# A new issue order for the first third of a fused recurrence and FFN kernel: decays of rounds 1 and 2 in quarters, no products of zeros

## The chip, the cores and the metric

The kernel runs on one core of one Trainium2 chip. The metric is the device time of one execution in microseconds (us). The time before is 322.89 us, the median of 3 runs.

## The reference

The first half is a gated linear recurrence in chunks of 32 positions; its result y, as 3072 rows of 256, goes through a two-layer FFN with a softplus between.

```
for c in range(nc):                                  # 24 chunks of 32
    cum = np.cumsum(la, axis=-1)                     # la = log(clip(a))
    L = np.exp(cum[..., :, None] - cum[..., None, :]) * causal
    y_intra = einsum('bhij,bhjd->bhid', einsum('bhin,bhjn->bhij', Cc, Bc) * L, xc)
    y_inter = einsum('bhin,bhnd->bhid', Cc, state) * exp(cum)[..., None]
    y[:, :, sl] = y_intra + y_inter
    state = decay_full * state + sum_j(Bc * xc * decay_from_j)
h = x @ w_in                                         # x: 3072 x 256, w_in: 256 x 2048
g = np.maximum(h, 0.0) + np.log1p(np.exp(-np.abs(h)))
return g @ w_out                                     # w_out: 2048 x 256
```

There are 4 batches, 8 heads, 768 positions, head dimension 32 and state dimension 16.

## The kernel before

The 768 positions are cut into 6 rounds of 128 (index u or j). A round holds 4 batches times 128 positions, that is 512 tokens, which is the width of one matmul. The FFN's hidden dimension of 2048 is cut into 16 tiles of 128 (index k). Each fp32 operand of the FFN is split into a high and a low part of type fp32r, and each product is made of three matmuls (high by high, high by low, low by high). So one step `F j.k` (first layer) is 6 matmuls of 512 columns, and one step `Z j.k` (second layer) is 6 as well; in 96 such pairs lies most of TensorE's work.

The recurrence of a round, for each half p of the batches: `D u.p` writes the decay weights into the tile `rm` (GpSimd, `affine_select`); `S u.p` makes the scores on TensorE (tile `sp`, 4 PSUM banks); `M u.p.q` multiplies a quarter of them into `rm` (VectorE); `I u.p` applies them to x (TensorE, tile `yp`). `B`, `U`, `N`, `T`, `C`, `R` scale, update and read the state (tiles `bp`, `zp`, `tb`, `td`, `cc`, `yp`). `G` multiplies by the growth factors `gg`, and `Xh`, `Xl` split the result into `xh`, `xl` for the FFN.

`W s` splits 512 KB of a weight matrix that `w s` has loaded: four operations of ScalarE and two of VectorE, in six stages, one each time the word stands in the order (even s: `w_in`, for the tiles k = s and s+1; odd s: `w_out`, tiles k = s-1 and s). `P j.k` takes a tile through softplus (`e`, ScalarE), its high part (`gh`, ScalarE) and its low part (`gl`, VectorE). `H0`, `H1` are the first halves of `F0.0` and `F0.1`. `ft`, `fr`, `gq`, `growth`, `gd`, `gg` prepare decay and growth factors: `growth` is made on chip, `gd` stores it to DRAM and `gg u` loads it back broadcast. `warm n` issues n matmuls of a zero tile (`some`), whose result nobody reads.

The order of the first third is written out by hand in `ORDER`, one word for each step. The instructions are kept in that order on each engine, and the DMAs on SP's queue as well. All compute engines take their instructions strictly in order, so a step that waits holds up everything behind it on its engine. After the words of `ORDER` a regular loop runs the steps s = 32 to 99, with the recurrence of rounds 3 to 5 put in by `FILLS`; the change does not touch it.

Buffers that matter: PSUM tiles of tag `ps` have 6 slots, shared by `sp` (4 at a time), `yp` (2), `zp`, `hp` and the small setup products; `rm` has 2 (`RM`), so the decays of round 1 wait for the `I` of round 0, and those of round 2 for the `I` of round 1; `wraw` has 4 (`WRAW`), so a later `w` waits for the third ScalarE stage of an earlier `W`; `un` has 2, so the load of round 3 waits for the readers of round 1.

The function `decays` takes a quarter k or none, so the change needs no new code:

```
ks = slice(0, KP) if k is None else slice(k * KP // 4, (k + 1) * KP // 4)
```

Of the kernel before, what the change touches and what calls it, by code (L numbers as in the profile page):

```python
# [55 lines left out]


ORDER = """
la warm1 warm1 loga loga gb warm4 logr logr ft0 ft0 gq0 gq0 ft0 ft0 ft0 growth D0.0.2 kb D0.0.3 growth ft0 fr0 fr0
warm1 us0.0 D0.0.1 D0.0.0 S0.0 w14 w6 M0.0.1 us0.1 warm1 D0.1.2 D0.1.1 W14 D0.1.3 M0.0.0 ux0.0 warm1 ft1 warm1 growth  # L60
w0 un1.0 M0.0.3 W14 ux0.1 w2 W6 W6 M0.0.2 W14 S0.1 W14 D0.1.0 M0.1.0 warm1 ft1 I0.0 D1.0 warm1 warm1 W14 W6 fr0 warm1
W14 W0 W0 M0.1.2 M0.1.1 fr1 w1 fr1 G0.0 gq1 fr1 W0 M0.1.3 ft1 W0 warm1 fr1 Xh0.0 ft1 Xl0.0 fr0 un1.1 gq1 I0.1 G0.1 W0
warm1 Xh0.1 W0 S1.0 tl W6 W6 Xl0.1 M1.0.0 warm1 M1.0.3 H0 W6 H1 F0.1 W2 W2 B0.0 F0.0 P0.1 M1.0.1 W2 M1.0.2 gd W2 P0.1
P0.1 F0.7 P0.0 W2 W2 P0.7 B0.1 w4 W4 F0.6 gg1 S1.1 C1 P0.0 D1.1 M1.1.2 P0.6 P0.0 F0.3 F0.2 M1.1.3 M1.1.0 W1 U0 P0.6 W1
w8 I1.0 warm1 W1 P0.3 M1.1.1 w3 N0 W1 W4 B1.0 B1.1 I1.1 warm1 gg3 W1 P0.6 w5 W1 W4 T1 W3 W4 W4 U1 W3 warm1 W3 w7 w10
R1 P0.2 Z0.0 G1.0 W4 W3 P0.3 P0.2 G1.1 W3 W3 Z0.1 F0.5 W5 F0.4 P0.2 P0.3 Xh1.1 W7 Xh1.0 F0.14 N1 W7 Z0.2 Xl1.1 Xl1.0
F1.2 W5 W5 P0.4 F1.1 un2.1 W5 w12 un3.1 W7 P0.4 P0.4 F1.4 gg2 W5 P0.5 P0.5 W7 F1.7 W5 P1.1 W7 W7 Z0.3 W12 F1.3 P0.5
W12 P0.7 P0.7 Z0.4 w11 Z0.5 W8 W8 W8 W12 P1.2 W8 Z0.6 F1.0 W12 P1.3 Z0.7 W12 P1.1 P1.1 W8 P1.0 F1.6 un3.0 K0.0 F1.5
P1.2 W8 P1.3 W10 W10 D2.0 P1.0 P1.0 w9 W10 W10 F0.8 K0.1 Z1.0 P1.6 W10 W10 Z1.1 P1.3 P1.2 P1.4 F0.10 P1.4 P1.5 P1.5
un2.0 C2 Z1.2 F0.9 B2.1 W11 Z1.3 P1.5 W12 P1.4 P1.6 P1.6 P0.9 P0.9 W9 P0.9 W11 W11 W11 T2 P0.10 P1.7 Z1.4 P0.8 Z1.5  # L70
Z1.6 P1.7 P1.7 F0.13 W9 W9 W9 S2.0 Z1.7 P0.8 P0.14 D2.1 W9 P0.10 F0.11 M2.0.1 F1.12 B2.0 W11 M2.0.0 P0.8 M2.0.3 P0.14
K1.1 W11 F1.10 w13 K1.0 P0.10 W9 W13 P1.10 w15 M2.0.2 P0.11 Z0.8 W13 W13 P0.14 Z0.9 W15 P0.11 P0.11 Z0.10 S2.1 M2.1.1
W13 P0.13 F0.15 W15 W15 F0.12 M2.1.0 P0.12 P0.12 P0.12 F1.15 P0.13 M2.1.2 Z0.11 W13 W15 P0.15 W15 P0.13 F1.8 P1.8
F1.11 W15 P1.10 W13 Z0.12 F1.9 P1.10 P0.15 Z0.13 P1.8 F1.14 P1.14 P1.8 P1.9 Z0.14 P0.15 P1.9 Z0.15 P1.9 P1.11 M2.1.3
U2 I2.0 E0 P1.14 P1.14 I2.1 R2 G2.1 Z1.8 Z1.9 G2.0 Z1.10 P1.12 P1.15 P1.12 P1.11 Xh2.0 P1.11 P1.12 Xh2.1 Xl2.1 Xl2.0
F1.13 P1.13 P1.15 N2 P1.15 Z1.11 P1.13 P1.13
"""
HALF = NFT // 2
AHEAD = 32
# [770 lines left out]
```

## Time and profile before

| | us |
|---|---|
| median of 3 runs | 322.89 |
| the profiled execution's own time | 322.9 |
| its span, first to last instruction | 320.8 |
| TensorE busy | 311.4 (97%) |
| ScalarE busy | 169.4 (53%) |
| VectorE busy | 165.3 (52%) |
| GpSimd busy | 33.8 (11%) |

Lines of the profile give an engine, the line of the kernel, the operation and its tiles as output<-inputs. PE is TensorE's matmuls, PEld its weight loads, DVE VectorE, ACT ScalarE, POOL GpSimd, SP the queue that issues the DMAs. Line 131 is the helper through which all instructions of the ordered part go, so the tiles tell them apart. Matmuls overlap, so a row's duration is longer than the distance to the next matmul. About 2.1 us of the time lie outside the span.

### The profile page before, as it was taken

The page shows a single profiled execution, that of the slowest core. Times are in us where ns is not written, and L with a number is a line of the kernel's source. Part 1 is how long each engine was busy: PE and PEld are TensorE (multiplying, and loading weights), DVE is VectorE, ACT ScalarE, POOL GpSimd, SP SyncE. Part 2 cuts the span into 40 slices and gives each one's busy share as a digit, 9 for nine tenths or more (in the row PEclk, how much of TensorE's full clock was granted, in tenths as well). Part 3 has the DMA queues.
Part 4 walks back from the last instruction along what each step waited for, and adds up shares of the span by engine and source line. Part 5 has one row for each costly group of instructions (what it writes and reads, how often), then busy time and mean ns, then how long its engine had stood idle before and what let it go on. Part 6 is the DMA issues. An engine that isn't in the chain of part 4 may idle for free.

```text
span 320.8 us, 5643 instructions
## 1 busy us (share of the span) xinstructions
PE 311.4 (97%) x2328; PEld 252.2 (79%) x2328; DVE 165.3 (52%) x254; ACT 169.4 (53%) x290; POOL 33.8 (11%) x35
## 2 busy tenths in 40 slices
PE   8989699999999999999999999999999999999996
PEld 5677478888888878888888888888888888888885
DVE  4899974474835793455762344372344342322222
ACT  5989398878764453443254534344633444544450
POOL 5730600000000230000410000230000000000000
PEclk9999999999999999999999999999999999999999
DMA  7968449611000242100250100000100000100001
GB/s 219 406 249 231 134 163 310 246 67 65 2 0 0 77 189 65 65 3 0 73 193 0 65 2 0 2 2 0 65 3 0 2 1 2 65 0 0 2 0 65
DMA packets 10297, 24.36 MB, mean 76 GB/s; under 512 B 1056, under 2 KB 1696, under 8 KB 10272
## 3 DMA queue, kind: packets, MB, share of 16 engines
q1 hardware_dynamic: 10272, 24.01, 21.6%
q8 instruction: 18, 0.29, 0.4%
q14 instruction: 7, 0.06, 0.0%
HBM read 20.76 MB, written 3.24 MB: 75 GB/s over the span
## 4 chain that ended last, share of the span: by engine, by line
PE 85%; DVE 10%; issue 2%; ACT 2%; POOL 1%; DVEq 0%; POOLq 0%; ACTq 0%
PE acc L131 38%; PE hp L131 37%; PE sp L131 3%; PE yp L131 3%; DVE gl L131 3%; DVE rm L131 1%; PE end L131 1%; DVE bp L400 1%; PE warm L131 1%; PE fp L131 1%; DVE w L131 1%; DVE bp L131 1%; DVE wil L131 1%; POOL kc L131 1%; PE gp L131 1%
## 5 line engine op out<-in xcount | busy, mean ns | idle before, releaser
L617 DVE TENSOR_TENSOR gl<-e,gh 128x512 fp32r<-128x512 f32 x62 | 42.9, 692 | 100.1 <-ACT gh L614 100.1
L611 ACT ACTIVATE e<-hp 128x512 f32<-128x512 f32 x62 | 37.1, 599 | 90.4 <-PE hp L131 90.0
L131 PE MATMUL hp<-xh,wil 128*128 128x512 f32 (+1 forms) x196 | 75.5, 385 | 1.1 <-DVE wil L131 1.1
L131 PE MATMUL hp<-xl,wih 128*128 128x512 f32 (+1 forms) x196 | 75.6, 386 | 0.3 <-DVE xl L131 0.3
L131 PE MATMUL hp<-xh,wih 128*128 128x512 f32 (+1 forms) x196 | 75.8, 387 | 0.0
L131 PE MATMUL acc<-gh,woh 128*128 128x512 f32 x188 | 74.7, 397 | 0.0
L131 PE MATMUL acc<-gh,wol 128*128 128x512 f32 x188 | 73.3, 390 | 1.1 <-DVE wol L131 1.1
L131 PE MATMUL acc<-gl,woh 128*128 128x512 f32 x188 | 73.5, 391 | 0.6 <-DVE gl L131 0.6
L131 PEld LDWEIGHTS hp<-xh,wil 128*128 128x128 f32 x196 | 36.8, 188 | 8.6 <-DVE wil L131 1.3
L131 PEld LDWEIGHTS hp<-xl,wih 128*128 128x128 f32 x196 | 36.8, 188 | 7.9 <-DVE xl L131 0.7
L131 PEld LDWEIGHTS hp<-xh,wih 128*128 128x128 f32 x196 | 36.8, 188 | 7.7 <-ACT xh L131 0.2
L131 PEld LDWEIGHTS acc<-gh,wol 128*128 128x128 f32 x188 | 35.3, 188 | 8.8 <-DVE wol L131 1.5
L131 PEld LDWEIGHTS acc<-gh,woh 128*128 128x128 f32 x188 | 35.3, 188 | 8.8 <-issue 0.9
L131 PEld LDWEIGHTS acc<-gl,woh 128*128 128x128 f32 x188 | 35.3, 188 | 8.0 <-DVE gl L131 1.0
L614 ACT CAST gh<-e 128x512 fp32r<-128x512 f32 x62 | 38.5, 621 | 5.2 <-PE acc L131 3.3
L131 DVE TENSOR_TENSOR gl<-e,gh 128x512 fp32r<-128x512 f32 x34 | 27.3, 814 | 23.8 <-ACT gh L131 23.7
L131 ACT ACTIVATE e<-hp 128x512 f32<-128x512 f32 x34 | 19.5, 590 | 18.4 <-PE hp L131 10.1
L131 POOL TENSOR_SCALAR_AFFINE_SELECT rm<-fc 128x512 f32<-128x512 f32 (+1 forms) x13 | 18.0, 1408 | 89.8 <-PE yp L131 84.5
L131 ACT CAST gh<-e 128x512 fp32r<-128x512 f32 x34 | 20.6, 617 | 7.3 <-PE acc L131 7.1
L131 ACT ACTIVATE signs<-wraw 128x512 f16<-128x512 f32 (+1 forms) x32 | 23.2, 775 | 0.0
L356 POOL TENSOR_SCALAR_AFFINE_SELECT rm<-fc 128x2048 f32<-128x2048 f32 x5 | 13.0, 2625 | 86.0 <-PE yp L131 86.0
L131 DVE TENSOR_TENSOR rm<-sp,rm 128x512 f32<-128x512 f32 x24 | 15.7, 680 | 2.5 <-PE sp L131 2.4
(93 smaller groups left out, 229.8 us busy)
## 6 DMA issues: line engine op xcount, KB each, us to landing
un<-in_un SPq DMA_DIRECT2D x10, 768.0 KB, 5.8
wraw<-in_w_in SPq DMA_DIRECT2D x8, 512.0 KB, 6.4
wraw<-in_w_out SPq DMA_DIRECT2D x8, 512.0 KB, 4.2
gg<-gd SPq DMA_DIRECT2D x20, 128.0 KB, 3.9
out_t<-o SPq DMA_DIRECT2D x9, 256.0 KB, 2.1
head_in_h<-in_un SPq DMA_DIRECT2D x2, 384.0 KB, 6.4
head_in_l<-in_un SPq DMA_DIRECT2D x2, 384.0 KB, 8.5
out_t<-half SPq DMA_DIRECT2D x2, 256.0 KB, 2.5
```

What stands on the lines that cost most here:

```text
L131: return lambda *a, **k: tc.keep_in_program_order(f(*a, **k))
L356: Pl.affine_select(out=weights_of(u, p)[:, ks].rearrange("p h (c i) -> p (h c) i", i=SUB), in_=fs.rearrange("p h c -> p (h c)").unsqueeze( ...
L400: V.tensor_tensor(bp, home(u, p)[:, U_B:].rearrange("p (h n) -> p h n", n=N), f_tok[u][0][:, p * KP : (p + 1) * KP].unsqueeze(2).broadcast ...
L611: A.activation(e, h, AF.Softplus)
L614: A.copy(gh, e)
L617: V.tensor_tensor(gl, e, gh.bitcast(F32), op=ALU.subtract)
```

## The change

Only the text of `ORDER` changes. Against the old one it has the same steps, with two differences in what is issued: the 17 `warm` words (20 matmuls of zeros) are all gone, and the four whole decays `D1.0`, `D1.1`, `D2.0`, `D2.1` are each replaced by four quarters, `D1.0.0` to `D2.1.3`. Everything else is permuted. The beginning and the stretch up to the first products of round 1's FFN, before and after:

```diff
-la warm1 warm1 loga loga gb warm4 logr logr ft0 ft0 gq0 gq0 ft0 ft0 ft0 growth D0.0.2 kb D0.0.3 growth ft0 fr0 fr0
-warm1 us0.0 D0.0.1 D0.0.0 S0.0 w14 w6 M0.0.1 us0.1 warm1 D0.1.2 D0.1.1 W14 D0.1.3 M0.0.0 ux0.0 warm1 ft1 warm1 growth
-w0 un1.0 M0.0.3 W14 ux0.1 w2 W6 W6 M0.0.2 W14 S0.1 W14 D0.1.0 M0.1.0 warm1 ft1 I0.0 D1.0 warm1 warm1 W14 W6 fr0 warm1
-W14 W0 W0 M0.1.2 M0.1.1 fr1 w1 fr1 G0.0 gq1 fr1 W0 M0.1.3 ft1 W0 warm1 fr1 Xh0.0 ft1 Xl0.0 fr0 un1.1 gq1 I0.1 G0.1 W0
-warm1 Xh0.1 W0 S1.0 tl W6 W6 Xl0.1 M1.0.0 warm1 M1.0.3 H0 W6 H1 F0.1 W2 W2 B0.0 F0.0 P0.1 M1.0.1 W2 M1.0.2 gd W2 P0.1
-P0.1 F0.7 P0.0 W2 W2 P0.7 B0.1 w4 W4 F0.6 gg1 S1.1 C1 P0.0 D1.1 M1.1.2 P0.6 P0.0 F0.3 F0.2 M1.1.3 M1.1.0 W1 U0 P0.6 W1
-w8 I1.0 warm1 W1 P0.3 M1.1.1 w3 N0 W1 W4 B1.0 B1.1 I1.1 warm1 gg3 W1 P0.6 w5 W1 W4 T1 W3 W4 W4 U1 W3 warm1 W3 w7 w10
-R1 P0.2 Z0.0 G1.0 W4 W3 P0.3 P0.2 G1.1 W3 W3 Z0.1 F0.5 W5 F0.4 P0.2 P0.3 Xh1.1 W7 Xh1.0 F0.14 N1 W7 Z0.2 Xl1.1 Xl1.0
...
+la loga loga ft0 logr us0.0 w0 logr gb ft0 kb S0.0 ux0.0 W0 growth gq0 us0.1 growth ux0.1 D0.0.0 W0 M0.0.0 ft0 D0.0.1
+W0 M0.0.1 D0.0.2 D0.0.3 M0.0.2 M0.0.3 D0.1.0 fr0 fr0 ft0 I0.0 ft0 D1.0.2 ft0 D0.1.2 gq0 W0 B0.0 D0.1.1 S0.1 w2 B0.1 U0
+G0.0 M0.1.0 gq1 fr1 M0.1.2 N0 M0.1.1 D0.1.3 M0.1.3 W0 ft1 W2 Xh0.0 fr0 D1.0.0 W0 fr1 un1.0 W2 I0.1 Xl0.0 gq1 G0.1 ft1
+w4 S1.0 D1.1.0 W2 fr0 W2 D1.1.2 ft1 W4 W4 M1.0.2 ft1 Xh0.1 w1 H0 H1 fr1 un1.1 w7 Xl0.1 W4 growth D1.0.1 B1.0 W2 W2 w6
+gd F0.1 fr1 D1.1.1 tl F0.0 F0.2 W4 P0.1 W4 P0.0 P0.2 M1.0.1 gg1 D1.0.3 B1.1 M1.0.3 M1.0.0 W4 F0.3 P0.0 S1.1 W1 P0.0 W1
+W6 W6 D1.1.3 w3 F0.5 W1 P0.1 W6 M1.1.1 F0.4 M1.1.0 P0.4 M1.1.3 M1.1.2 U1 W1 C1 W6 P0.1 I1.0 D2.0.0 W1 W6 w5 W1 I1.1 R1
+Z0.0 G1.1 W3 D2.1.0 W3 D2.1.1 P0.2 G1.0 D2.0.2 P0.2 Z0.1 P0.3 D2.0.3 un2.0 W6 W3 W3 P0.5 w12 S2.0 M2.0.0 un2.1 Xh1.0
+W7 W7 W3 M2.0.2 F0.7 W3 D2.1.2 W7 W7 un3.1 P0.3 P0.3 P0.4 F0.6 Xh1.1 W5 Xl1.0 Z0.2 D2.1.3 W5 W5 Xl1.1 T1 P0.5 P0.6 N1
...
```

## Rows read from the trace of the kernel before

**Rows 1.** The page, engines' busy time, then TensorE in 40 slices and its granted clock

```profile
PE 311.4 (97%) x2328; PEld 252.2 (79%) x2328; DVE 165.3 (52%) x254; ACT 169.4 (53%) x290; POOL 33.8 (11%) x35
...
PE   8989699999999999999999999999999999999996
...
PEclk9999999999999999999999999999999999999999
```

**Rows 2.** The chain that ended last, in order of time: start, duration

```profile
46.96 5.53 PE hp L131 x23
...
59.29 1.36 PE hp L131 x6
...
118.19 2.79 PE acc L131 x11
```

**Rows 3.** TensorE's waits in the first 125 us: total, times, longest

```profile
PE zp L131 <- DVE bp L131: 1.6, 1, 1.6
PE hp L131 <- DVE wil L131: 1.1, 1, 1.1
PE acc L131 <- DVE wol L131: 1.1, 1, 1.1
...
PE acc L131 <- DVE gl L131: 0.6, 1, 0.6
...
PE hp L131 <- DVE xl L131: 0.3, 1, 0.3
```

**Rows 4.** TensorE in order of time, 0 to 47 us: start, duration, count

```profile
0.98 3.17 PE L131 MATMUL warm<-some 128*32 128x512 bf16 x6 [0.98 <-POOL some L131]
4.18 1.53 PE L131 MATMUL fp<-both_logs,kc 128*128 128x96 f32 x8
...
9.16 1.13 PE L131 MATMUL fp<-both_logs,kc 128*128 128x96 f32 x8
...
19.16 0.39 PE L131 MATMUL hp<-xh,wih 128*128 128x256 f32 x1
...
30.36 0.43 PE L131 MATMUL zp<-head_in_h,bp 128*32 128x64 f32 x16
...
36.62 0.50 PE L131 MATMUL acc<-gh,woh 128*128 128x512 f32 x1
```

**Rows 5.** All products of zeros, by their tile: nanoseconds, least/median/most

```profile
L131 PE MATMUL warm<-some x20: 376/390/631, 1.0 to 35.3; 128*32 128x512 bf16 x20
```

**Rows 6.** GpSimd and VectorE in order of time, 6 to 37 us

```profile
6.23 5.59 POOL L131 TENSOR_SCALAR_AFFINE_SELECT rm<-fc 128x512 f32<-128x512 f32 x8 [1.69 <-ACT fc L131]
...
8.56 2.48 DVE L131 TENSOR_TENSOR rm<-sp,rm 128x512 f32<-128x512 f32 x4 [1.30 <-PE sp L131]
...
17.76 2.40 POOL L131 TENSOR_SCALAR_AFFINE_SELECT rm<-fc 128x2048 f32<-128x2048 f32 x1 [1.67 <-DVE xl L131]
18.36 2.33 DVE L131 TENSOR_TENSOR wil<-w,wih 128x512 fp32r<-128x512 f32 x1
...
32.04 5.20 POOL L131 TENSOR_SCALAR_AFFINE_SELECT rm<-fc 128x2048 f32<-128x2048 f32 x2 [11.88 <-PE yp L131]
32.05 2.93 DVE L131 TENSOR_TENSOR bp<-un,ft 128x256 f32<-128x256 f32 x2
...
34.90 2.86 DVE L131 TENSOR_TENSOR gl<-e,gh 128x512 fp32r<-128x512 f32 x1
```

**Rows 7.** A group of instructions by line: total us, mean ns of one, idle before

```profile
L617 DVE TENSOR_TENSOR gl<-e,gh 128x512 fp32r<-128x512 f32 x62 | 42.9, 692 | 100.1 <-ACT gh L614 100.1
```

**Rows 8.** DMA: the store of the growth factors and two others, KB, us to landing

```profile
wraw<-in_w_out SPq DMA_DIRECT2D x8, 512.0 KB, 4.2
...
out_t<-half SPq DMA_DIRECT2D x2, 256.0 KB, 2.5
...
gd<-both_logs SPq DMA_DIRECT2D x1, 96.0 KB, 8.8
```

**Rows 9.** Busy time of PE, PEld, DVE, ACT, POOL in one stretch (instructions), clock, DMA

```profile
40.00:48.00 8.00, 7.69 (x34) 6.03 (x33) 6.19 (x11) 8.00 (x15) 0.00 (x0) 1.00 0.48 164
```

More of the change, by code (lines that the diff above doesn't have):

```diff
@@ L64 @@
-P0.1 F0.7 P0.0 W2 W2 P0.7 B0.1 w4 W4 F0.6 gg1 S1.1 C1 P0.0 D1.1 M1.1.2 P0.6 P0.0 F0.3 F0.2 M1.1.3 M1.1.0 W1 U0 P0.6 W1
-w8 I1.0 warm1 W1 P0.3 M1.1.1 w3 N0 W1 W4 B1.0 B1.1 I1.1 warm1 gg3 W1 P0.6 w5 W1 W4 T1 W3 W4 W4 U1 W3 warm1 W3 w7 w10
-R1 P0.2 Z0.0 G1.0 W4 W3 P0.3 P0.2 G1.1 W3 W3 Z0.1 F0.5 W5 F0.4 P0.2 P0.3 Xh1.1 W7 Xh1.0 F0.14 N1 W7 Z0.2 Xl1.1 Xl1.0
-F1.2 W5 W5 P0.4 F1.1 un2.1 W5 w12 un3.1 W7 P0.4 P0.4 F1.4 gg2 W5 P0.5 P0.5 W7 F1.7 W5 P1.1 W7 W7 Z0.3 W12 F1.3 P0.5
-W12 P0.7 P0.7 Z0.4 w11 Z0.5 W8 W8 W8 W12 P1.2 W8 Z0.6 F1.0 W12 P1.3 Z0.7 W12 P1.1 P1.1 W8 P1.0 F1.6 un3.0 K0.0 F1.5
@@ L69 @@
[L69 to L73, printed above, removed]
@@ L74 @@
-F1.11 W15 P1.10 W13 Z0.12 F1.9 P1.10 P0.15 Z0.13 P1.8 F1.14 P1.14 P1.8 P1.9 Z0.14 P0.15 P1.9 Z0.15 P1.9 P1.11 M2.1.3
-U2 I2.0 E0 P1.14 P1.14 I2.1 R2 G2.1 Z1.8 Z1.9 G2.0 Z1.10 P1.12 P1.15 P1.12 P1.11 Xh2.0 P1.11 P1.12 Xh2.1 Xl2.1 Xl2.0
-F1.13 P1.13 P1.15 N2 P1.15 Z1.11 P1.13 P1.13
+la loga loga ft0 logr us0.0 w0 logr gb ft0 kb S0.0 ux0.0 W0 growth gq0 us0.1 growth ux0.1 D0.0.0 W0 M0.0.0 ft0 D0.0.1
+W0 M0.0.1 D0.0.2 D0.0.3 M0.0.2 M0.0.3 D0.1.0 fr0 fr0 ft0 I0.0 ft0 D1.0.2 ft0 D0.1.2 gq0 W0 B0.0 D0.1.1 S0.1 w2 B0.1 U0
@@ new lines @@
+W7 W7 W3 M2.0.2 F0.7 W3 D2.1.2 W7 W7 un3.1 P0.3 P0.3 P0.4 F0.6 Xh1.1 W5 Xl1.0 Z0.2 D2.1.3 W5 W5 Xl1.1 T1 P0.5 P0.6 N1
+W5 W5 w13 Z0.3 P0.5 W7 F1.3 W5 P0.4 W7 P0.7 w8 F1.1 P0.7 P0.6 W8 F1.0 w9 P0.7 Z0.4 P1.1 W8 W8 P1.3 W12 W12 P0.6 F1.5
+w10 M2.0.3 P1.1 W12 Z0.5 P1.0 W12 W12 Z0.6 D2.0.1 M2.0.1 W12 P1.1 F1.4 Z0.7 P1.3 F1.6 P1.0 gg2 F1.2 W10 P1.0 P1.3 W8
+W10 F1.7 K0.1 W10 W10 W10 K0.0 W10 W9 w14 P1.2 P1.2 P1.4 P1.7 Z1.0 P1.4 Z1.1 F0.12 w11 P1.2 Z1.2 P1.4 W8 Z1.3 W8 W14
+W9 P1.6 P1.5 P1.6 P1.5 P1.7 P1.5 Z1.4 F0.10 W14 W14 gg3 Z1.5 P1.6 P0.10 P0.10 W14 W14 P1.7 P0.12 F0.8 W14 F0.9 W9 Z1.6
@@ new lines @@
+Z1.7 S2.1 P0.10 P0.8 W11 W9 B2.0 W11 P0.12 M2.1.2 P0.9 M2.1.1 F0.11 K1.1 W11 P0.8 K1.0 W11 W9 P0.8 W9 F0.14 F0.13 Z0.8
+P0.9 P0.13 W13 P0.12 W13 W13 W11 P0.9 Z0.9 W13 P0.11 B2.1 F0.15 P0.13 W11 W13 F1.8 P0.14 w15 W15 F1.13 W15 M2.1.3
+F1.10 P0.13 P0.11 P0.11 W13 Z0.10 Z0.11 M2.1.0 P0.14 F1.9 P1.9 Z0.12 Z0.13 P0.15 P0.15 P1.9 T2 P0.14 C2 P1.13 F1.14
+un3.0 W15 P1.9 W15 F1.15 F1.12 W15 W15 P1.14 Z0.14 P0.15 F1.11 Z0.15 P1.8 P1.14 P1.14 I2.0 P1.8 P1.8 P1.10 P1.10 P1.10
+U2 P1.11 I2.1 R2 E0 G2.0 Z1.8 G2.1 N2 Z1.9 P1.11 P1.11 Xh2.0 Xl2.0 P1.12 P1.13 P1.13 Z1.10 Z1.11 Xh2.1 P1.12 P1.12
@@ L77 @@
+P1.15 P1.15 Xl2.1 P1.15
 """
```

## The prediction

> **What bounds the kernel now.** I read the page first, then the chain that ended last, then TensorE's waits, then TensorE's own order of time, and last the two engines that its waits name. TensorE is busy in 97% of the span, and every slice from 40 us on is full [rows 1]. The chain says the same: from 46.96 us to the end it is products, one after the other, but for one pause near 118 us [rows 2], which the waits give as 0.6 us [rows 3]. So behind 47 us the time is the sum of TensorE's products, which the change keeps. Time can be won only before, and what a new order is worth is what TensorE does there other than useful products.
>
> I count that between its first useful product at 4.18 us and the chain's solid run at 46.96 us: 42.8 us. Useful work, each step as the distance from its first matmul to the next step's: from 4.18 to 19.16 us the setup products, two scores and two `I` of round 0 and the first scores of round 1 make 11.2 of 15.0 us; from 19.16 to 30.36 us two `F` in halves (2.9), four whole `F` at 1.36 [rows 2] and one `S` of 1.1 make 9.4 of 11.2; from 30.36 to 36.62 us `U0`, `I1`, `U1`, `R1` make 3.8 of 6.3; from 36.62 us three `F`, three `Z` and one further matmul make 8.4 of 10.3 [the stretches' edges are in rows 4]. That is 32.8 us. The other 10.0 us are 14 products of zeros (20 less the six ahead of 4.18 us [rows 4, 5], 0.3 to 0.4 us each), four waits of 1.1, 1.6, 1.1 and 0.3 us for VectorE [rows 3], and short gaps where the kind of product changes.
>
> Those waits have one cause that the rows show. A whole decay on GpSimd takes 2.4 us, and a VectorE operation whose inputs all lie in SBUF and that meets it takes as long: `wil` 2.33 us at 18.36, two `bp` 2.93 together at 32.05, a `gl` 2.86 at 34.90 [rows 6], where such an operation alone takes 0.69 [rows 7]. The three waits over 1 us stand right behind these.
>
> **The change part by part.** The sum is made against the profiled execution's 322.9 us, which is the median.
>
> Products of zeros. The six before 4.18 us cost nothing, since TensorE then waits for the logarithms anyway. The other 14 go: at most 14 x 0.38 = 5.3 us, but only where TensorE was not about to wait in any case. What they may have bought is the clock. The first products of zeros take about 0.6 us and later ones 0.38 to 0.39 [rows 5]; the first group of `fp` takes 1.53 us and the second, equal one 1.13 [rows 4]. The granted clock reads full speed in every slice [rows 1], so that row does not show the rise; the durations do: the lower of the two levels until about 4.5 us, with the six products of zeros before it. After the change nothing runs ahead of `fp`, so I take the lower level for `fp` and `S0.0`. Price from above: both doubled, 1.1 + 1.1 us; from below 0, as the four `M0.0` behind them also wait for GpSimd's quarters, eight in 5.59 us [rows 6]. I take 0.7, since with these quarters starting at 6.3 us the fourth is there at about 9.2 and covers most of it.
>
> The Trainium skill, page "TensorE: Matmul & The Clock Gate", Part 1, says that the lower clock is the default, that sustained activity lifts it, and that idling brings it back. The rise that the durations show agrees; no row here shows a fall. By that rule a sparse beginning could stay at the lower level, which is a rival below.
>
> Decays in quarters. A quarter takes 5.59/8 = 0.70 us, four 2.8 against 2.4 to 2.6: GpSimd has room, being 11% busy [rows 1]. A VectorE operation that meets one waits at most 0.7 in place of 2.2. But the eight quarters of round 2 follow one another from `I1.0` on, and VectorE has `P0.1`, `W1`, `P0.2`, `W6`, `W3` parts among them, so several operations may each wait once. Bounds: 0, if `G1` and `M2` (which read PSUM; the `M` in the eight quarters above ran four in 2.48 us [rows 6]) stand opposite, and 6 x 0.7 = 4.2 us of VectorE time. Only what reaches TensorE counts: the last stage of `W1` before `Z0.0`, and `M2.0.0`, which frees the bank for `F0.6`. I take 0.7 + 0.8 = 1.5 us, the two of six that something waits for.
>
> The quarter `D1.0.2` stands ahead of three quarters of `D0.1` on GpSimd and waits for `I0.0`; behind it are `M0.1.2`, `M0.1.1`, `M0.1.3` and `I0.1`. Three or four quarters are 2.1 to 2.8 us behind `I0.0`, less than the VectorE work that `M0.1.3` has ahead of it (some eight operations at 0.6, 4.8 us), so it costs 0.
>
> The new order. I follow the engines' queues by the rows' durations. `S0.0` starts near 6.6 us, `M0.0` ends near 10.4 and `I0.0` near 11.3 (12.4 to 13.2 before). `S0.1` needs four PSUM slots and gets the last when ScalarE has read `gp0`, near 11.9. `M0.1.3` ends near 15.9, `I0.1` near 17.1, `S1.0` near 18.2, `H0` starts at 18.5. `H1` waits for a slot until `M1.0.2`, `F0.1` for `Xl0.1` near 20.6, and `F0.0` ends near 22.0 (23.48 before). Useful until then: 14.6 us, so 22.0 - 4.15 - 14.6 = 3.25 us are lost. From there to `Z0.4` I find 24.5 us of products in 24.9, so 0.4 lost, with little in hand: ScalarE feeds them, at 0.53 to 0.6 us an operation and no rest (in 40 to 48 us before, 15 operations fill all 8.0 [rows 9]). To this come gaps where the kind of product changes: before, 10.0 - 5.3 - 4.1 leaves 0.6 us for them, and the products of zeros covered others; I take 0.9 us in place of the 0.4 and the gaps together.
>
> Sum lost after: 3.25 + 0.9 + 0.7 (clock) + 1.5 (quarters) = 6.4 us, against 10.0 before. Saved 3.6 us: 322.9 - 3.6 = 319.3 us. The pause of 0.6 us near 118 us stays: it comes from the whole decays of round 3, which the loop issues as before.
>
> The queue of SP. `growth`'s last stage moves behind `W4`'s third on ScalarE, from about 9 us to about 20.5; so `gd` goes out there, the four `gg1` wait for it to land, and `w3`, `w5`, `un2.0` stand behind them. At 2.5 us to land (an output of similar kind) `w3` goes out near 26 and is there 4.2 us later [rows 8], near 30.5, and `W3` asks for it near 32: cost 0. At 8.8 us, its time before, it is a rival. I take the low value, since before it was issued at 12.6 us behind the first loads, and by 21 us these should have landed.
>
> **The rivals.** (1) The store lands late: 8.8 us [rows 8] puts `gg1` at 29.5, `w3` at 32, its landing at 36; ScalarE, which has no slack there, stands 4 us: 319.3 + 4 = 323.3 us, level. For it speaks the row, against it the emptier DMA at that time. Chance 0.17.
>
> (2) The new order meets nothing: no price for the clock (-0.7), none for the quarters (-1.5), half of the 3.25 us filled: -3.8, so 315.5 us, and 312.9 if all 10.0 us went. For it speaks that the waits before come from whole decays alone, and that both prices have a lower bound of 0; against it, that the slots of PSUM and the strict queues leave real waits in the first 20 us. Chance 0.21.
>
> (3) The other side: the clock stays at the lower level until TensorE has a dense stretch, which first comes with `F0.0` and `F0.2` near 22 us. Then those products that are on the path double: `I0.0` 0.9, `S0.1` 1.1, `gq1` 0.9, `I0.1` 1.1, `S1.0` 1.1 and the halves 2.9, together 8.0 us, in place of 0.7: 319.3 + 7.3 = 326.6 us. It decides against the forecast as soon as it costs 3.6 us more, that is, if it lasts past `I0.1`; if it lasts past `R1`, another 4 us, it is 330.6 us, over 2% slower. For it speaks that the useful products fill only 11.2 of the first 15 us; against it, that this is still a busy engine. This is the page's rule above at its strongest. Chance 0.12.
>
> That the change doesn't do what it says can't well be: the words are read straight into instructions.
>
> **How the numbers follow.** Forecast 0.50, (1) 0.17, (2) 0.21, (3) 0.12. A measurement of this kernel tells about 2% (6.5 us) from no change. Faster by more, below 316.4 us: most of (2) and a little of the forecast, whose own prices spread over 317 to 322: 0.21. Slower by more, above 329.4: a third of (3), and mishaps, 0.05. The rest, 0.74, within. The range goes from 314.5 (most of (2)) to 325.0 (all of (1), the mild part of (3)), leaving out about 0.15.
>
> **What would show it.** `I0.0` near 11.3 us and the first `hp` near 18.5: the order's first part. First `fp` and `sp` groups slower than 1.13 and about 1.2 us, later ones not: the clock as priced; `sp` of round 1 slow as well: rival (3). VectorE operations of 1.2 to 1.4 us beside GpSimd's quarters, none above 2 before 100 us: the decays. The wait of SP for `gd`, and of ScalarE for `wraw`: rival (1). TensorE's solid run should begin with about 6.4 us lost instead of 10.0, and the distance from the first product of round 2's FFN to the end should be the same as before. If that distance differs, my whole account is wrong, since it rests on nothing changing behind the ordered part.

## The result, and the profile after

The changed kernel takes 319.51 us, the median of 4 runs (318.35 to 320.14), against 322.89 for the kernel before in the same comparison, the median of its three undisturbed runs (322.82 to 323.71; a fourth took 627.74 us and is left out). The ratio of the means is 0.9884, with a 95% interval of 0.9844 to 0.9923: faster by 3.8 us, or 3.4 by the medians, less than the 2% that the prediction took as the limit. In the later comparisons the kernel before took anything from 320.1 to 324.9 us, with medians of 322.45 to 322.9, so one or two microseconds between two single executions say little. The forecast was 319.3 us. The total is right, but it is the sum of two errors that cancel, and the rows below show both.

The profiled execution took 319.56 us, with a span of 317.9. On the page TensorE's share is 97% as before, and GpSimd has 12 more instructions, the quarters. The granted clock now has one lower digit, in the slice from 111 to 119 us, where [rows 1] have none.

```profile
PE 307.7 (97%) x2308; PEld 252.9 (80%) x2308; DVE 160.9 (51%) x254; ACT 169.0 (53%) x290; POOL 38.7 (12%) x47
...
PEclk9999999999999979999999999999999999999999
```

TensorE's waits (total, times, longest). The three waits over 1 us of [rows 3] are gone; the one for `gl`, which was 0.6, is now 1.9.

```profile
PE fp L131 <- ACT both_logs L131: 4.2, 1, 4.2
PE acc L131 <- DVE gl L131: 1.9, 1, 1.9
PE hp L131 <- DVE rm L131: 0.5, 1, 0.5
```

TensorE in order of time (start, duration), to be read beside [rows 4]:

```profile
4.21 2.00 PE L131 MATMUL fp<-both_logs,kc 128*128 128x96 f32 x8 [4.21 <-ACT both_logs L131]
6.14 2.09 PE L131 MATMUL sp<-head_in_h 32*128 32x128 f32 x32
...
10.26 1.45 PE L131 MATMUL yp<-rm,head_in_h 128*32 128x128 f32 x32 [0.30 <-DVE rm L131]
...
14.43 1.11 PE L131 MATMUL fp<-both_logs,kc 128*128 128x96 f32 x8
...
16.83 1.18 PE L131 MATMUL sp<-un 32*128 32x128 f32 x32
...
18.18 0.37 PE L131 MATMUL hp<-xh,wih 128*128 128x256 f32 x1
...
21.59 0.40 PE L131 MATMUL hp<-xh,wih 128*128 128x512 f32 x1
...
106.03 1.10 PE L131 MATMUL yp<-cc,tb 32*64 32x128 f32 x32
...
111.27 0.39 PE L131 MATMUL acc<-gh,woh 128*128 128x512 f32 x1
113.61 0.50 PE L131 MATMUL acc<-gl,woh 128*128 128x512 f32 x1 [1.95 <-DVE gl L131]
...
114.77 0.63 PE L131 MATMUL acc<-gh,wol 128*128 128x512 f32 x1
...
117.75 0.47 PE L131 MATMUL hp<-xh,wih 128*128 128x512 f32 x1
```

Four rows of the kernel before answer to the late ones, in the same view: its `R2`, the start of `F1.13`, the product that waits for `gl`, and its first product of round 2's FFN.

```profile
110.45 1.10 PE L131 MATMUL yp<-cc,tb 32*64 32x128 f32 x32
...
115.69 0.39 PE L131 MATMUL hp<-xh,wih 128*128 128x512 f32 x1
...
118.19 0.50 PE L131 MATMUL acc<-gl,woh 128*128 128x512 f32 x1 [0.64 <-DVE gl L131]
...
120.82 0.39 PE L131 MATMUL hp<-xh,wih 128*128 128x512 f32 x1
```

**Where the time went.** `R2` starts at 106.03 in place of 110.45, 4.42 us earlier, and the new order has by then also done `F1.13`, which the old one still has to do (1.36 us). So 5.8 us are won up to there. But the first product of round 2's FFN comes at 117.75 in place of 120.82, only 3.07 us earlier: 2.7 us are given back between 106 and 118 us. From that product to the end of the span it is 200.15 us, before 199.98: nothing changes behind.

**The late loss** has two parts. The wait for `gl` grows from 0.64 to 1.95 us: 1.3. And the 11 `acc` products from the end of that wait take 113.61 to 117.75, 4.14 us, where the same 11 took 2.63 before (118.19 to 120.82): 1.5.

The wait has not grown because `gl` comes later. From the start of `R2` to the product that waits for it are 7.74 us before (110.45 to 118.19) and 7.58 after (106.03 to 113.61). What is gone is work for TensorE in between: the old order has `F1.13` there, 1.36 us, and the new one has done it ahead of `R2`. So of the 5.8 us won up to `R2`, these 1.36 come back as a longer wait.

For the second part, busy time by engine in two stretches (PE, PEld, DVE, ACT, POOL, each with its count, then the granted clock):

```profile
111.00:113.00 2.00, 0.66 (x3) 0.20 (x2) 2.00 (x7) 2.00 (x5) 0.00 (x0) 1.00 0.83 342
...
115.00:117.00 2.00, 2.00 (x6) 1.40 (x6) 1.66 (x3) 0.62 (x1) 0.00 (x0) 0.50 0.07 11
```

TensorE stands still for 1.95 us, and shortly after the granted clock goes from 1.00 to 0.50, from the 2.4 to the 1.2 GHz level, with a busy TensorE under it. The Trainium skill, page "TensorE: Matmul & The Clock Gate", Part 1, says that idling brings the lower level back; the trace agrees, here after one pause, though the page would not lead one to expect it after so short a one. In the one of the four runs whose mean clock was 1.000 instead of 0.995 the time is 318.35 us, 1.1 to 1.8 us under the others, about this second part. Not all of the 1.5 us is the clock: in runs 4 and 6 below the clock stays at 1.00, and the same 11 products take 3.07 us. So the clock costs 1.07 us here, and 0.44 are mostly a second, short wait for a `gl` among them.

VectorE in the same time shows what `gl` waits behind:

```profile
105.12 1.28 DVE L131 TENSOR_TENSOR half<-acc,half 128x512 f32<-128x512 f32 x2
106.32 3.92 DVE L400 TENSOR_TENSOR bp<-un,ft 128x256 f32<-128x256 f32 x2
110.16 1.28 DVE L131 TENSOR_TENSOR gg<-yp,gg 128x512 f32<-128x512 f32 x2
...
112.88 0.68 DVE L131 TENSOR_TENSOR gl<-e,gh 128x512 fp32r<-128x512 f32 x1
```

and GpSimd:

```profile
104.93 2.53 POOL L131 TENSOR_SCALAR_AFFINE_SELECT rm<-fc 128x2048 f32<-128x2048 f32 x1 [66.18 <-PE yp L131]
107.42 2.56 POOL L356 TENSOR_SCALAR_AFFINE_SELECT rm<-fc 128x2048 f32<-128x2048 f32 x1
```

The two `bp` of round 3 read SBUF alone and last as long as the two whole decays of round 3 beside them, to 110.2 us; the `half` just ahead, which read PSUM, run at their usual speed. An operation that goes through the pinned order carries line 131; the `bp`, at line 400 of their own function, do not. They come from the loop's `FILLS`, in the part that the build is free to place once the pinned part ends (`PINNED = 34`, the step of the loop up to which the order is kept), and it placed both ahead of the `gl` for which TensorE stands. The kernel before has the same operations ahead of it; the only `gl` between its two `bp` is that of another tile (`P1.14`).

### The profile page after: what moved, and what is told of

It reads as the page before. It is cut to its first block, busy times and chain, and to the rows that moved or that the text cites. A ratio compares the mean times of both kernels' runs of the same rounds, so it can differ in the third digit from the quotient of the medians.

```text
span 317.9 us, 5610 instructions
## 1 busy us (share of the span) xinstructions
PE 307.7 (97%) x2308; PEld 252.9 (80%) x2308; DVE 160.9 (51%) x254; ACT 169.0 (53%) x290; POOL 38.7 (12%) x47
## 4 chain that ended last, share of the span: by engine, by line
PE 92%; DVE 5%; DMA 1%; issue 1%; ACT 1%; DVEq 0%; ACTq 0%
PE acc L131 40%; PE hp L131 40%; PE sp L131 4%; PE yp L131 4%; DVE bp L400 1%; PE fp L131 1%; PE end L131 1%; DMA both_logs<-in_alr 1%; PE zp L131 1%; DVE rm L131 1%; DVE gg L131 0%; DVE wil L131 0%; DVE w L131 0%; PE gp L131 0%; DVE half L131 0%
## 5 line engine op out<-in xcount | busy, mean ns | idle before, releaser
L617 DVE TENSOR_TENSOR gl<-e,gh 128x512 fp32r<-128x512 f32 x62 | 42.9, 691 | 100.1 <-ACT gh L614 100.1
L131 DVE TENSOR_TENSOR gl<-e,gh 128x512 fp32r<-128x512 f32 x34 | 22.9, 688 | 22.1 <-ACT gh L131 22.1
L131 POOL TENSOR_SCALAR_AFFINE_SELECT rm<-fc 128x512 f32<-128x512 f32 (+1 forms) x25 | 22.9, 949 | 80.0 <-PE yp L131 76.2
L131 ACT ACTIVATE signs<-wraw 128x512 f16<-128x512 f32 (+1 forms) x32 | 24.2, 783 | 0.0
```

Of the source, the lines that this page charges most:

```text
L131: return lambda *a, **k: tc.keep_in_program_order(f(*a, **k))
L617: V.tensor_tensor(gl, e, gh.bitcast(F32), op=ALU.subtract)
```

## The experiments

None of the kernels leaves out any of the computation; products of zeros give a result that nobody reads. Kernels made from the one before have `ORDER` on one line, so their helper is line 114. The account to test: (A) the late wait is VectorE's order at the end of the pinned part together with the whole decays of round 3, and the clock falls because TensorE stands still. Rivals: the clock falls because the zeros are gone, or the early gain is the zeros' and not the quarters'.

**1. The late loss: another place for the loop's work.** The pinned part is made eight steps longer:

```diff
-PINNED = 34
+PINNED = 42
```

> The new kernel with the loop kept in program order up to step 42 in place of 34, which moves the two bp, cc and td of round 3 on VectorE behind the last gl of the ordered part; nothing else is issued otherwise. Theory A (5.8 us were won ahead of 104 us, and 2.7 given back between 104 and 118 us, since gl of P1.11 stands behind two bp that meet the whole decays of round 3, and the clock falls after that wait): the wait of TensorE for gl near 112 us goes from 1.9 to under 0.5 us, the granted clock stays at full, and the time falls by 2 to 3 us against the changed kernel, to 316.5 to 317.5 us. Rival B (the wait comes from somewhere else, ScalarE for instance, and the clock falls by itself): the wait and the time stay, 319 to 320 us.

Measured: 316.06 us (315.80 to 316.36), ratio 0.9796 [0.9771, 0.9822], under the changed kernel by 3.45 us in the medians and 2.8 in the ratios, a little better than expected. From `R2` to round 2's first FFN product are 8.18 us (106.41 to 114.59) in place of 11.72. VectorE's order of time has no `bp` ahead of the `gl`:

```profile
107.55 1.29 DVE L131 TENSOR_TENSOR gg<-yp,gg 128x512 f32<-128x512 f32 x2 [0.77 <-PE yp L131]
...
109.84 0.87 DVE L131 TENSOR_TENSOR gl<-e,gh 128x512 fp32r<-128x512 f32 x1 [0.49 <-ACT gh L131]
```

and the stretch from 115 us is full, at the full clock:

```profile
115.00:117.00 2.00, 2.00 (x10) 1.62 (x10) 0.00 (x0) 0.80 (x2) 0.00 (x0) 1.00 0.40 121
```

The whole decays are still there, so it takes both: a long decay, and `bp` placed beside it ahead of something that TensorE waits for.

**2. The late loss: the other half of the pair.** Round 3's decays, and all later ones, in quarters; the placement is left free.

```diff
-    (-16, "D@.0 un@+.0 un@+.1 gg@+"),
-    (-11, "S@.0 M@.0.0 M@.0.1 M@.0.2 M@.0.3 D@.1"),
+    (-16, "D@.0.0 D@.0.1 D@.0.2 D@.0.3 un@+.0 un@+.1 gg@+"),
+    (-11, "S@.0 M@.0.0 M@.0.1 M@.0.2 M@.0.3 D@.1.0 D@.1.1 D@.1.2 D@.1.3"),
```

> The new kernel with the decays of rounds 3 to 5 in quarters too; VectorE's order stays. Theory A: the two bp near 106 us take 1.1 to 1.3 us each in place of 3.9 together, gl is ready 1.3 us or more earlier, the wait near 112 us falls under 0.7 us and the clock stays: 317 to 318 us. Rival B: no change, 319 to 320 us. The later rounds should not matter in either, since TensorE never waits there.

Measured: 317.06 us (316.88 to 317.47), ratio 0.9831 [0.9802, 0.9860]. VectorE: the two `bp` stand at the same place and take 1.26 us in place of 3.92, and the late wait is 0.5.

```profile
106.25 1.26 DVE L400 TENSOR_TENSOR bp<-un,ft 128x256 f32<-128x256 f32 x2
...
111.33 0.68 DVE L131 TENSOR_TENSOR gl<-e,gh 128x512 fp32r<-128x512 f32 x1
```

So either half of the pair, taken away, removes most of the loss. Neither run issues products of zeros, and the clock stays up in all ten executions of the two (0.999 or 1.000), so their absence alone does not bring it down.

**3. The clock alone.** Six products of zeros are put into the pause, ahead of `Z1.11`, and the wait left as it is. The zeros get a tile of their own, and their result a slot of PSUM.

```diff
-P1.13 P1.13 Z1.10 Z1.11 Xh2.1 P1.12 P1.12
+P1.13 P1.13 Z1.10 warm6 Z1.11 Xh2.1 P1.12 P1.12
...
-    some = p2.tile([P, 512], F32, tag="o0", name="some", bufs=1)[:, :16].bitcast(BF16)
+    some = cp.tile([P, 16], F32, name="some")[:].bitcast(BF16)
```

> The new kernel with six products of zeros put in front of Z1.11, where TensorE waits 1.9 us; the zeros get a tile and PSUM slots of their own. They fill about 1.3 us of the wait and free nothing. Theory A, its second half (the clock falls because TensorE stands still there): the wait itself stays as long, counted from the end of Z1.10 to the gl product, but the products behind it keep 0.39 us and full clock: 1.5 us less, about 318 us. Rival B (the clock falls by itself at that place): clock 0.5 again near 115 us, 319.5 us or a little more.

Measured: 320.68 us (320.55 to 320.75), ratio 0.9937 [0.9916, 0.9958], slower than the changed kernel although the clock stayed at 1.000. The chain in order of time gives it away: all through the FFN six products take 1.37 us in place of 1.36. Its first and last piece of one stretch:

```profile
256.46 1.37 PE hp L131 x6
...
308.64 1.37 PE hp L131 x6
```

The same stretch of the changed kernel:

```profile
255.96 1.36 PE hp L131 x6
...
307.64 1.36 PE hp L131 x6
```

Between the starts lie 38 pieces of six: 52.18 / 228 = 228.9 ns a product against 51.68 / 228 = 226.7. Over the 1152 FFN products that is 2.5 us. What differs in that stretch is where the tiles lie in SBUF, since the new tile shifts others. So the run's time does not price the clock, and the next run keeps the places.

**4. The same, with every tile at its place.** The zeros lie in a tile of 32 bytes a partition that the kernel already has, unused (`apart`).

```diff
-    cp.tile([P, 8], F32, name="apart")
+    some = cp.tile([P, 8], F32, name="apart")[:].bitcast(BF16)
...
-P1.13 P1.13 Z1.10 Z1.11 Xh2.1 P1.12 P1.12
+P1.13 P1.13 Z1.10 warm6 Z1.11 Xh2.1 P1.12 P1.12
```

> As the run with late zeros before, but the tile of zeros lies in the 32 bytes a partition of the unused tile apart (so the products of zeros have 16 columns of weights in place of 32), and no other tile changes its place in SBUF. In the run before, each product of the FFN came 228.9 ns after the last in place of 226.7, in all stretches. If that came from the shifted tiles, it is 226.7 again; then by theory A (the clock falls because TensorE stands still near 112 us) the time is 1 to 1.5 us below the new kernel's, 318 to 318.5 us. If the zeros themselves make products slower, 320 to 321 us again.

Measured: 318.69 us (318.30 to 319.65), ratio 0.9888 [0.9845, 0.9932]. The chain's spacing is 226.7 ns again, TensorE fills the pause with zeros, and the clock is 1.00 from 112 to 120 us:

```profile
111.22 1.47 PE L131 MATMUL warm<-apart 128*16 128x512 bf16 x6
...
113.46 0.50 PE L131 MATMUL acc<-gl,woh 128*128 128x512 f32 x1 [0.34 <-DVE gl L131]
...
116.53 0.39 PE L131 MATMUL hp<-xh,wih 128*128 128x512 f32 x1
```

`gl` itself comes hardly sooner (112.73 us against 112.88). From `R2` to round 2's first FFN product are 10.65 us (105.88 to 116.53) in place of 11.72, and the span is 1.3 us shorter. The 1.07 us are the clock's part. By the medians it is 0.8, but the two sets of runs overlap. That the clock fell because TensorE stood still rests on all the runs: where the pause was left as it is (the changed kernel, runs 6 and 11) the mean clock was 0.995 or lower in 9 of 18 executions, where it was filled or removed (runs 1 to 4 and 12) in none of 27. Run 6 has other waits too, at which its clock may have fallen; without it, it is 5 of 8. The slower products of run 3 were the places' doing; which tile matters stays open.

**5. The early gain: quarters alone.** The kernel before, zeros kept, with only its four whole decays cut, each at its old place:

```diff
-... I0.0 D1.0 warm1 warm1 W14 ...
+... I0.0 D1.0.0 D1.0.1 D1.0.2 D1.0.3 warm1 warm1 W14 ...
```

> The old kernel with the four decays of rounds 1 and 2 in quarters at the places where the whole ones stood, zeros kept. If the whole decays cost the three waits of 1.1, 1.6 and 1.1 us: 2 to 4 us less, 319 to 321 us, and no VectorE operation over 1.5 us before 100 us. If the quarters only spread the same waiting over more operations: within 1 us, 322 to 324 us.

Measured: 318.48 us (318.39 to 320.13), ratio 0.9900 [0.9851, 0.9949], against 322.6 before: 4.1 us by the medians and 3.2 by the ratio, which the interval does not tell from the whole change (0.9884). Of the waits of [rows 3] only small ones are left:

```profile
PE acc L114 <- DVE gl L114: 0.7, 1, 0.7
PE hp L114 <- DVE xl L114: 0.6, 2, 0.4
```

`R2` starts at 106.30, 4.15 us earlier than before, and the first product of round 2's FFN at 116.67, also 4.15 earlier: nothing is given back, since here `F1.13` stands at its old place. These are two single executions; run 9 shows that about 2 us of the 4.15 are not there in every one.

**6. The new order without quarters.** Each whole decay stands where its quarter 0 stood.

```diff
-... Xh0.0 fr0 D1.0.0 W0 fr1 un1.0 ... D1.1.0 W2 fr0 W2 D1.1.2 ...
+... Xh0.0 fr0 D1.0 W0 fr1 un1.0 ... D1.1 W2 fr0 W2 ...
```

> The new kernel with the decays of rounds 1 and 2 whole again, each at the place of its quarter 0. If the quarters are needed by the new order: VectorE operations of 2.3 to 2.9 us at 17 to 22 and 31 to 36 us come back, and 2 to 4 us are lost, 321.5 to 323.5 us. If the order alone does it: within 1 us of 319.5 us.

Measured: 320.63 us (320.53 to 325.31, three of ten runs at 325.3 with a mean clock of 0.989), ratio 1.0002 [0.9957, 1.0048]. One of the three waits over 1 us comes back, behind a `wol` of 2.86 us, and one for `rm` grows from 0.5 us:

```profile
PE hp L114 <- DVE rm L114: 1.5, 1, 1.5
PE acc L114 <- DVE wol L114: 0.9, 1, 0.9
```

In its profile the late pause is 1.95 us again, and the clock stays at 1.00 behind it:

```profile
115.46 0.50 PE L114 MATMUL acc<-gl,woh 128*128 128x512 f32 x1 [1.95 <-DVE gl L114]
...
118.53 0.40 PE L114 MATMUL hp<-xh,wih 128*128 128x512 f32 x1
```

On the new order the quarters are worth 1.1 us by the medians and 3.8 by the ratios, which count the executions with the fallen clock. The time lies between the two that were expected. The order without them is worth at most 2 us, and by the interval perhaps nothing.

**7. The zeros alone.** The kernel before without its 17 `warm` words, nothing else.

> The old kernel with all its words for products of zeros taken out and nothing else. My count has 14 of them, 5.3 us, behind 4.18 us. If they lay on the path: 4 to 5 us less, 318 to 319 us. If TensorE would have waited in their place for VectorE, as the dense VectorE row says: 0 to 1.5 us less, 321.5 to 323 us; then the new order, not the zeros, is what won. If the clock is then at the lower level for long: 324 us or more.

Measured: 324.76 us (321.58 to 326.41, ten runs), ratio 1.0066 [1.0027, 1.0105]: slower by 2 us. The runs differ by the mean clock: 321.6 at 1.000, 324.7 to 324.8 at 0.994 or 0.995, 325.4 to 326.4 at 0.989 or below. In the profile (of the longest of the ten runs, 326.41 us) TensorE's wait for `bp` is 2.0 us and that for `wil` 1.6, and the granted clock drops around such waits, as from 40 to 44 us:

```profile
40.00:44.00 4.00, 3.79 (x9) 3.02 (x10) 3.30 (x7) 3.55 (x7) 0.00 (x0) 0.50 0.02 4
```

**8. Zeros out, quarters in, old order.** With run 5 this prices the zeros where no long wait is left.

> The old order with the quarters, and without any products of zeros: both differences of the change in what is issued, without its new order. The zeros alone taken out cost 2 us, with the clock at the lower level near 22 and 36 to 48 us, behind waits of 1.6 and 2.0 us. If the zeros only guard the clock across such waits, and the quarters remove the waits, they can go at no cost: 317.5 to 319 us, clock full in every stretch behind 8 us. If they are needed for the clock even so: 320 to 322 us and a lower clock somewhere between 12 and 48 us. Against the new kernel's 319.5 us this also says what its new order is worth.

Measured: 320.39 us (318.94 to 321.49), ratio 0.9950 [0.9918, 0.9982], 1.9 us over run 5, and the granted clock reads 1.00 in every stretch up to 48 us. So neither expectation holds: the time is that of the second, without its lower clock. In the profile `R2` starts at 109.12 us, 2.82 later than in run 5. The beginning shows part of it: `S0.0` takes 1.51 us in place of 1.19, two waits are new, and with a third, for `xl`, 0.8 us are lost by the end of `F0.0` (23.34 us against 22.55).

```profile
11.64 1.17 PE L114 MATMUL sp<-head_in_l 32*128 32x128 f32 x32 [0.94 <-DMA head_in_l<-in_un]
...
15.36 1.16 PE L114 MATMUL gp<-kc,logs 128*128 128x128 f32 x8 [0.93 <-DVE rm L114]
```

The other 2.0 us are not the zeros' doing; the next runs show them with the zeros too.

**9 and 10. The old order pinned longer,** as in run 1, with the quarters: with the zeros, and without them.

> The old order with its products of zeros, the quarters, and the loop in program order up to step 42. Against 318.5 us without the last: 0.5 to 0.8 us less by theory A, 317.7 to 318 us. Against the run without zeros it says whether the zeros win or cost once the long waits are gone: equal within 0.5 us if they fill time that TensorE stands anyway, up to 2 us slower if they lie on the path.

> The run before with the loop in program order up to step 42: the same late repair as in the first run, on the old order. The old order's wait near 118 us was 0.6 to 0.7 us and no clock fell behind it, so by theory A the repair is worth 0.5 to 0.8 us here: 317 to 318 us, against 316.1 on the new order, which would then be worth 1 to 2 us once its late wait is gone. If the new order is worth nothing: 316 us.

Measured: 317.73 us (317.61 to 319.35), ratio 0.9866 [0.9819, 0.9912], with the zeros; 320.13 (318.00 to 321.24), ratio 0.9903 [0.9873, 0.9934], without, where 317 to 318 was expected. Neither has a late wait. From `R2` to round 2's first FFN product the longer pinning gives 1.0 us on the old order, with zeros (10.37 to 9.33) and without (10.34 to 9.33), and 3.5 on the new one (11.72 to 8.18), where it removes the longer pause and what follows it.

Up to the end of run 5's pinned part run 9 issues the same instructions, and still its profile (319.35 us, the longest of its four runs) has `R2` at 108.29 us, 1.99 later. Until 31 us the two agree within 0.05. Then the two `bp` on VectorE and the eight quarters of round 2 on GpSimd begin together. In run 5 VectorE goes ahead and GpSimd is held:

```profile
31.24 0.75 DVE L114 TENSOR_TENSOR bp<-un,ft 128x256 f32<-128x256 f32 x2
...
31.14 10.50 POOL L114 TENSOR_SCALAR_AFFINE_SELECT rm<-fc 128x512 f32<-128x512 f32 x8 [9.48 <-PE yp L114]
```

In run 9 GpSimd's quarters are done 3.2 us sooner, and VectorE is held at each of six operations:

```profile
31.20 1.77 DVE L114 TENSOR_TENSOR bp<-un,ft 128x256 f32<-128x256 f32 x2
32.90 1.19 DVE L114 TENSOR_TENSOR gl<-e,gh 128x512 fp32r<-128x512 f32 x1
...
31.10 7.32 POOL L114 TENSOR_SCALAR_AFFINE_SELECT rm<-fc 128x512 f32<-128x512 f32 x8 [9.48 <-PE yp L114]
```

Runs 8 and 10 were profiled in the second form as well (their `bp` 1.78 and 1.77 us). Compared with run 9, which has it too, their `R2` is only 0.8 us later (109.12 and 109.08): that is what the zeros are worth in these executions, not 1.9. The times of these four kernels fall into two groups 1.7 to 2.2 us apart, which is likely the same thing; without zeros the longer times are 12 of 20, with them 2 of 8. Why one form or the other comes about is not settled. The seven profiles of the new order with quarters show one form only there: eight quarters in 7.5 to 7.6 us beside a `wol` of 1.19 or 1.20.

With the pause gone the new order, which has no zeros, is by the medians 4.1 us better than the old without zeros, and 1.7 better than the old with them; against the shorter times of each it is 2.0 and 1.6.

**11. Early zeros for the clock at the start.** The changed kernel with the first six products of zeros put back:

```diff
-la loga loga ft0 logr us0.0
+la warm1 warm1 warm4 loga loga ft0 logr us0.0
```

> The new kernel with the six products of zeros of the old beginning put back at the beginning, and no others. If the clock at the beginning costs what I priced, 0.7 us: fp back from 2.0 to 1.5 us, the first sp from 2.1 to 1.2, the first I about 0.6 us earlier, and 0.5 to 0.9 us less in all, 318.6 to 319 us. If GpSimd's quarters, the load of the weights and the queues cover it: the products are faster, the first F starts at the same time, 319.5 us. If all of the slower products lie on the path: 1.9 us or more, 317.6 us.

Measured: 318.75 us (318.30 to 319.00), ratio 0.9880 [0.9851, 0.9910], 0.76 under the changed kernel. In the profile the first group runs at the upper level, and the first `hp` comes at 16.64 us, 1.54 earlier:

```profile
4.15 1.11 PE L131 MATMUL fp<-both_logs,kc 128*128 128x96 f32 x8
```

Of the 1.54 us 1.04 are left at `R2` (104.99 us). The late pause is there as before (1.9 us), and the clock falls behind it to 0.67 from 112 to 116 us.

**12. Runs 1 and 11 together,** the version that they point to.

> The new kernel with both repairs: the loop in program order up to step 42 and the six products of zeros at the beginning. If the two prices are separate, the gains add: by theory A 2 to 3 us and 0.5 to 0.9, together 316 to 317 us. If the second only moves the beginning against other waits: as with the first alone.

Measured: 315.90 us (314.98 to 316.64), ratio 0.9806 [0.9767, 0.9844], the fastest median of all, but only 0.16 under run 1. Its profile shows why:

```profile
4.14 2.00 PE L131 MATMUL fp<-both_logs,kc 128*128 128x96 f32 x8
```

With the same six products of zeros ahead the first group took the lower level's time in this run, so the rise is not certain; why stays open. The spread of its runs, from 314.98, may be this.

## Why the prediction was right, point by point

- **The total** (319.3 against 319.51) is right by luck, because an early gain that was forecast too small and a late loss that was not foreseen cancel: 3.6 forecast, 5.8 early less 2.7 late in the traces.
- **The beginning.** `I0.0` was forecast near 11.3 us and came at 10.26, the first `hp` 18.5 against 18.18, the end of `F0.0` 22.0 against 21.59. With the price of the clock, 3.25 + 0.7 = 3.95 us were to be lost up to there; it is 21.59 - 4.21 - 14.6 = 2.8.
- **The clock at the start.** `fp` and `S0.0` take 2.00 and 2.09 us, later groups 1.11 and 1.18: both doubled, the upper bound of the term. Run 11 gets 0.76 us back in the medians, whose runs overlap, and 1.04 at `R2` in the traces, so the 0.7 had about the right size. Rival 3 asked for a slow `sp` of round 1 as well; at 16.83 it is not.
- **The quarters.** VectorE operations beside them take 0.9 to 1.2 us, forecast 1.2 to 1.4, and none is above 2 before 100 us, for example this one against 2.33 in [rows 6]:

```profile
20.88 1.19 DVE L131 TENSOR_TENSOR wil<-w,wih 128x512 fp32r<-128x512 f32 x1
```

- The term itself was mis-sized: 1.5 us for quarters and 0.9 for gaps were to be lost behind `F0.0`, and what is left of the loss up to `R2` is 10.0 - 5.8 - 2.8 = 1.4 for both. From the end of `F0.0` to 100 us the list of waits has one of 0.5 us, for `rm`, at 23.84 us. Run 5 shows what the term hid: the quarters are the larger part of the gain, not a price on it. And "waits at most 0.7" takes VectorE as the one that is held; in run 5 it is GpSimd, and that is worth 2 us.
- **The zeros.** "At most 5.3 us" of gain was the wrong way to look at them: the old order without them takes 2 us more by the medians, in run 7 with the clock lower, and 0.8 in like executions with the quarters (runs 8 to 10). They fill time in which TensorE waits anyway; the new order bears their loss.
- **SP's queue.** `gd` goes out at 20.12 us, as forecast near 20.5, and `gg1` 2.7 us later, not 8.8 [rows 8]. Rival 1 is refuted.

```profile
20.12 0.34 SPq L140 DMA_DIRECT2D gd<-both_logs  x1
22.80 1.75 SPq L140 DMA_DIRECT2D gg<-gd  x4
```

- **The step that failed:** "The pause of 0.6 us near 118 us stays: it comes from the whole decays of round 3, which the loop issues as before." The decays are issued as before and `gl` is ready as long after `R2` as before, but a pause is also set by what the waiting engine has left to do. The new order moves `F1.13`, 1.36 us of products, ahead of `R2`, so the pause became 1.95 us, and the clock put 1.07 us on top. Run 1 shows both gone together, run 4 the second alone.
- **Rival 2** (315.5 us, nothing met) came nearer in the early part. With the late loss removed, run 1 takes 316.06.
- **The distance** from round 2's first FFN product to the end, by which the whole account was to be judged, is the same within 0.2 us.

## What to carry to other kernels

A step that a new order does early is missing where it stood: when such a change is priced, ask of each later wait what filled the time ahead of it, and follow the operations that a scheduler places freely up to the next engine that waits. If it does wait, pin them too. Cut a long GpSimd operation before searching for an order around it: with the old order, that one edit won about as much as the new order and the cut together. When two engines can hold each other up, profile more than one execution before their difference is put down to an edit. When a tile is added for an experiment, compare the spacing of the same products with the run without it before the result is read.

## What was not expected of the hardware

- One pause of TensorE of 1.95 us, amid dense products, brought the granted clock to 0.50 for some 3 us, in three of four runs by their mean clock of 0.995. It cost 1.07 us. With the pause filled or absent the profiles show 1.00 there (runs 1, 2 and 4); in run 6's profile it stayed 1.00 behind an equal pause, so the fall is likely, not certain.
- The granted clock reads 1.00 at the start even where `fp` takes 2.00 us in place of 1.11: there the durations tell the level, not the row.
- The same FFN products follow each other in 226.7 or 228.9 ns by where tiles lie in SBUF (runs 3 and 4), 2.0 us of this kernel's time by their medians.
- A whole decay of 2.5 us holds a VectorE operation that reads SBUF alone for as long as it lasts, while one that reads PSUM beside it runs on unhindered. It can also go the other way: in run 5 a quarter on GpSimd, 0.70 us alone, took 3.57 us while six VectorE operations ran at their usual speed (the two `bp` 0.75 together); in run 9, with the same instructions at nearly the same times, VectorE was held. That is 2 us between two executions of one order, with the clock at 1.00 in both.
